# Batch 0 of a linear-attention kernel: keys and q loaded ahead of all values, E and F as f32 over two hardware queues

## Chip, cores and metric

One core of one Trainium2 chip. The metric is the device time of one execution in microseconds (us). The kernel before takes 522.49 us (median of six runs in the rounds of the comparison; 522.26 in the three runs known when the prediction was made).

## The reference, cut to what matters

```python
k_proj = einsum('ks,bhsd->bhkd', E, k)          # E: 64 x 1024; k: 8 batches, 8 heads, 1024 x 64
v_proj = einsum('ks,bhsd->bhkd', F, v)
scores = (1 / sqrt(64)) * q @ k_proj^T          # 1024 x 64 for each head
attn   = softmax(scores)
x      = (attn @ v_proj), heads side by side    # 8192 x 512
h = x @ w_in                                    # 512 -> 2048
out = (h * clip(h + 3, 0, 6) / 6) @ w_out       # 2048 -> 512
```

The two large products (w_in, w_out) are nearly all of the work. Batch b + 1's attention is woven into the large products of batch b; only the attention of batch 0 has nothing to hide behind.

## The kernel before: the parts concerned

Heads are handled in four pairs. `busy(n)` is n matmuls of ones on ones, whose result nobody reads: fillers, meant to keep TensorE's clock up.

```python
ef_raw = consts.tile([P, S], bf16, name="ef_raw")
nc.gpsimd.dma_start(out=ef_raw[:KP], in_=E)            # f32 in memory, cast to bf16 on the way
nc.gpsimd.dma_start(out=ef_raw[KP:], in_=F)
# (cut) table load, ones
busy(8)
for n, j in (("k", 0), ("q", 0), ("v", 0), ("k", 1), ("q", 1), ("k", 2), ("q", 2), ("v", 1),
             ("k", 3), ("q", 3), ("v", 2), ("v", 3)):
    nc.gpsimd.dma_start(out=kqv[0][n][:, 2 * j:2 * j + 2], in_=kqv_dram[n][0][:, 2 * j:2 * j + 2])
# (cut) w_in, k/q/v of batch 1, w_out follow on the same queue
for so in range(SO):                                    # E and F turned, 128 rows together
    nc.tensor.transpose(ef_ps[:, so * P:(so + 1) * P], ef_si[:, so, :], ident)
nc.vector.tensor_copy(ef_t[0], ef_pv[:, 0])             # E's half; F's half by ScalarE
# (cut)
def by_pairs(self):
    keys(0)                                             # project, copy to kp
    self.q_out(0, self.q_transpose(0, pat)); self.keys_transposed(0, 2)
    busy(2); self.scores(0, pmm); busy(3)               # scores: matmuls, then exp on ScalarE
    vals(0)(); keys(1)
    self.q_out(1, self.q_transpose(1, pat))
    lns = logs(0, both)                                 # sums of exp (matmuls), ln on ScalarE
    self.keys_transposed(2, 2); busy(1)
    self.scores(1, pmm)
    recs = inverses(lns)                                # exp(-ln): behind the next pair's exp
    av = self.values(0, pat, both); busy(3)             # attn @ v_proj
    # (cut) pairs 2 and 3 alike: values of pair j - 1 or j - 2 between keys and scores of pair j
    rest = [vals(2)]; av = self.values(2, pat, one); out(2, av, recs)
    recs = inverses(logs(3, one)); rest.append(vals(3)); busy(1)
    av = self.values(3, pat, one); out(3, av, recs)     # x of the last pair
    for copy in rest: copy()
    busy(4)                                             # then the first large product
```

The softmax here doesn't subtract the row's maximum and nothing guards it: scores larger than these inputs give would overflow.

## Time and profile before

| | kernel before |
|---|---|
| median of 6 runs (lowest, highest) | 522.49 us (521.59, 522.92) |
| span of the profiled run, granted clock | 520.9 us, 0.999 |
| TensorE busy | 506.9 us, 97% |
| first keys projected | 7.20 us |
| first large matmul (the plateau) | 28.11 us |
| from there to the end of the span | 492.8 us |

Most lines that carry the reading are in the prediction. One more, the scores of the last pair, is the row of the old order with which the changed kernel is compared below:

```profile
23.41 0.41 PE L196 MATMUL mm<-qTp,kT 64*64 64x256 bf16 x8
```

The busy tenths of VectorE and of the DMA engines in slices of 13 us show that VectorE has room in the first two slices (1 and 5 tenths busy) while the loads fill their engines (8 and 9):

```profile
DVE  1568636444363453554454354534525544444420
...
DMA  8999993993049711695119931298111110011112
```

### The profile page before, as it was taken

The page shows a single profiled execution, that of the slowest core. Times are in us where ns is not written, and L with a number is a line of the kernel's source. Part 1 is how long each engine was busy: PE and PEld are TensorE (multiplying, and loading weights), DVE is VectorE, ACT ScalarE, POOL GpSimd, SP SyncE. Part 2 cuts the span into 40 slices and gives each one's busy share as a digit, 9 for nine tenths or more (in the row PEclk, how much of TensorE's full clock was granted, in tenths as well). Part 3 has the DMA queues.
Part 4 walks back from the last instruction along what each step waited for, and adds up shares of the span by engine and source line. Part 5 has one row for each costly group of instructions (what it writes and reads, how often), then busy time and mean ns, then how long its engine had stood idle before and what let it go on. Part 6 is the DMA issues. An engine that isn't in the chain of part 4 may idle for free.

```text
span 520.9 us, 7264 instructions
## 1 busy us (share of the span) xinstructions
PE 506.9 (97%) x2806; PEld 225.1 (43%) x2858; DVE 238.5 (46%) x378; ACT 283.9 (55%) x517; POOL 36.3 (7%) x55
## 2 busy tenths in 40 slices
PE   6899999999999999999999999999999999999996
PEld 3444444444444444444444444444444444444443
DVE  1568636444363453554454354534525544444420
ACT  2677485676446654568437664466635664444431
POOL 7620000100020000200002000200000000000000
PEclk9999999999999999999999999999999999999999
DMA  8999993993049711695119931298111110011112
GB/s 131 203 207 207 207 181 117 190 151 97 22 77 211 145 43 42 117 196 121 42 30 170 176 81 42 63 204 168 42 40 32 40 42 28 34 42 41 40 42 81
DMA packets 67443, 53.95 MB, mean 104 GB/s; under 512 B 29776, under 2 KB 59216, under 8 KB 67408
## 3 DMA queue, kind: packets, MB, share of 16 engines
q0 software_dynamic: 30016, 29.63, 35.6%
q1 hardware_dynamic: 37248, 23.73, 17.3%
q8 instruction: 22, 0.36, 0.3%
q10 hardware_dynamic: 144, 0.13, 0.1%
q14 instruction: 13, 0.11, 0.1%
HBM read 59.24 MB, written 16.78 MB: 146 GB/s over the span
## 4 chain that ended last, share of the span: by engine, by line
PE 94%; DMA 2%; issue 1%; DVE 1%; POOL 1%; ACT 1%; DVEq 0%; ACTq 0%; POOLq 0%
PE mm L393 43%; PE mm L402 41%; PE at L210 3%; PE at L150 3%; DMA q<-in_q_dram 2%; PE at L196 1%; PE mm L84 1%; PE at L180 1%; DVE qTp L187 0%; DVE xT L232 0%; DVE vp L162 0%; PE mm L210 0%; PE mm L196 0%; ACT aT L201 0%; POOL k L95 0%
## 5 line engine op out<-in xcount | busy, mean ns | idle before, releaser
L397 DVE SCALAR_TENSOR_TENSOR g<-r,mm 128x512 bf16<-128x512 f32 x256 | 173.4, 686 | 218.6 <-ACT r L396 218.4
L393 PE MATMUL mm<-xT,w_in_sb 128*128 128x512 bf16 x1000 | 233.1, 380 | 2.6 <-issue 1.9
L402 PE MATMUL mm<-w_out_sb,g 128*128 128x512 bf16 x999 | 230.1, 380 | 1.5 <-issue 0.3
L396 ACT ACTIVATE r<-mm 128x512 f32<-128x512 f32 x256 | 152.3, 603 | 62.6 <-PE mm L393 61.3
L393 PEld LDWEIGHTS <-w_in_sb 128*128 128x128 bf16 x1024 | 96.8, 98 | 125.6 <-issue 14.1
L402 PEld LDWEIGHTS <-g 128*128 128x128 bf16 x1024 | 98.9, 98 | 119.4 <-issue 2.2
L416 ACT COPY o_sb<-mm 128x512 f32<-128x512 f32 x63 | 36.9, 586 | 147.6 <-PE mm L402 144.7
L232 DVE TENSOR_TENSOR xT<-at,rec 128x512 bf16<-128x512 f32 x56 | 38.2, 684 | 16.5 <-ACT rec L228 15.4
L228 ACT ACTIVATE rec<-ln 128x512 f32<-128x512 f32 x64 | 40.4, 640 | 0.1
L223 ACT ACTIVATE ln<-at 128x512 f32<-128x512 f32 x59 | 32.7, 617 | 2.4 <-PE at L210 2.3
L201 ACT ACTIVATE aT<-at 128x512 bf16<-128x512 f32 x56 | 29.2, 612 | 0.9 <-PE at L196 0.9
L358 POOL COPY mark<-kT 1x1 bf16<-1x1 bf16 x5 | 0.9, 177 | 276.4 <-DMA kT<-kp 276.4
L150 PE MATMUL at<-k,ef_t 128*64 128x512 bf16 (+1 forms) x88 | 15.9, 323 | 1.1 <-DMA k<-in_k_dram 1.1
L150 PE MATMUL at<-v,ef_t 128*64 128x512 bf16 (+1 forms) x88 | 15.9, 324 | 0.0
L150 PEld LDWEIGHTS <-ef_t 128*64 128x64 bf16 x176 | 9.6, 109 | 11.4 <-issue 5.9
L162 DVE CAST vp<-at 64x512 bf16<-64x512 f32 (+1 forms) x21 | 11.3, 541 | 4.0 <-PE at L150 3.0
L210 PE MATMUL at<-aT,vp 64*64 64x512 bf16 x112 | 12.3, 379 | 0.5 <-DVE vp L162 0.4
L210 PE MATMUL at<-aT,ones 64*64 64x512 bf16 x118 | 12.7, 400 | 0.0
L84 PE MATMUL mm<-ones 128*128 128x512 bf16 x31 | 10.9, 446 | 1.6 <-DVE ones L77 1.5
L157 DVE CAST kp<-at 64x512 bf16<-64x512 f32 (+1 forms) x21 | 10.2, 522 | 4.3 <-PE at L150 4.3
L210 PEld LDWEIGHTS <-ones 64*64 64x64 bf16 x128 | 3.9, 103 | 13.4 <-issue 13.1
L196 PEld LDWEIGHTS <-kT 64*64 64x64 bf16 x256 | 5.8, 106 | 8.0 <-issue 5.1
(44 smaller groups left out, 94.8 us busy)
## 6 DMA issues: line engine op xcount, KB each, us to landing
out_dram<-o_sb SPq DMA_DIRECT2D x63, 256.0 KB, 2.0
q<-in_q_dram POOLq DMA_DIRECT2D x7, 1024.0 KB, 9.5
k<-in_k_dram POOLq DMA_DIRECT2D x7, 1024.0 KB, 15.0
v<-in_v_dram POOLq DMA_DIRECT2D x7, 1024.0 KB, 19.9
w_out_sb<-in_moe_w_out_dram POOLq DMA_DIRECT2D x4, 512.0 KB, 27.7
w_in_sb<-in_moe_w_in_dram POOLq DMA_DIRECT2D x3, 512.0 KB, 12.6
k<-in_k_dram POOLq DMA_DIRECT2D x4, 256.0 KB, 8.1
q<-in_q_dram POOLq DMA_DIRECT2D x4, 256.0 KB, 8.6
```

The costliest lines, as they stand in the source:

```text
L84: nc.tensor.matmul(ps, ones[:, :P], ones, start=True, stop=True)
L150: nc.tensor.matmul(ps[e * KP:(e + 1) * KP], ef_t[e][:, so, :], kqv[self.b]["kv"[e]][:, hs, so, :], start=(so == 0), stop=(so == SO - 1))
L201: nc.scalar.activation(self.aT[j][:, r].rearrange("p a n -> p (a n)"), tiles[r], AF.Exp, scale=scale)
L210: nc.tensor.matmul(tiles[t][c:c + D].rearrange("p (r n) -> p r n", r=2), stationary(r, 2 * j + a), self.aT[j][r:r + KP, :, a, :], start=Tr ...
L223: nc.scalar.activation(ln, den, AF.Ln)
L228: nc.scalar.activation(rec, ln, AF.Exp, scale=-1.0)
L232: nc.vector.tensor_mul(self.xT[:, j, t, :], av, rec)
L393: nc.tensor.matmul(h_ps, w_in_sb[:, ko, fo * P:(fo + 1) * P], xT[:, ko, t, :], start=(ko == 0), stop=(ko == KO - 1))
L396: nc.scalar.activation(r, h_ps, AF.Relu, bias=0.5, scale=1.0 / 6.0)
L397: nc.vector.scalar_tensor_tensor(g[:, fo, :], r, 1.0, h_ps, op0=ALU.min, op1=ALU.mult)
L402: nc.tensor.matmul(o_ps, g[:, fo, c * P:(c + 1) * P], w_out_sb[:, fo, :], start=(fo == 0), stop=(fo == FO - 1))
L416: nc.scalar.copy(o_sb, o_ps)
```

## The change

Its intent: TensorE should get through keys, q, scores and sums of all pairs as fast as the loads come, with values and products behind; and E and F should leave GpSimd's queue, so that every casting load starts earlier. Cut to its core:

```diff
-    ef_raw = consts.tile([P, S], bf16, name="ef_raw")
-    nc.gpsimd.dma_start(out=ef_raw[:KP], in_=E)
-    nc.gpsimd.dma_start(out=ef_raw[KP:], in_=F)
+    ef_f32 = consts.tile([P, S], f32, name="ef_f32")
+    nc.sync.dma_start(out=ef_f32[:KP], in_=E)
+    nc.scalar.dma_start(out=ef_f32[KP:], in_=F)
-    busy(8)
+    busy(12)
-    for n, j in (("k", 0), ("q", 0), ("v", 0), ("k", 1), ... ("v", 2), ("v", 3)):
+    for n, j in [(n, j) for j in range(KO) for n in ("k", "q")] + [("v", j) for j in range(KO)]:
+    nc.vector.tensor_copy(ef_raw[:, :S // 2], ef_f32[:, :S // 2])
+    nc.scalar.copy(ef_raw[:, S // 2:], ef_f32[:, S // 2:])
     # by_pairs, new body (the old one is cut)
+            for j in range(KO):
+                keys(j)
+                if j > 0: self.scores(j - 1, pmm)
+                busy(1)
+                self.keys_transposed(2 * j, 2)
+                self.q_out(j, self.q_transpose(j, pat))
+                busy(1)
+                if j > 0:
+                    den = self.sums(j - 1, pmm, ts)          # ts: both halves for pair 0, else one
+                    lns = {t: self.log(den[t]) for t in ts}
+                    recs[j - 1, 0] = reciprocal(lns[0], opool, "o_sb")
+                    ...                                      # and recs[0, 1] for pair 0
+                    busy(1)
+            self.scores(KO - 1, pmm)
+            for j in range(KO):
+                copy = vals(j); copy(0); ...                 # second copy at once for pair 0, else later
+                av = self.values(j, pat, range(NB) if j == 0 else (0,))
+                self.scaled(j, 0, av[0], recs[j, 0])
+                busy(1)
+                ...                                          # j == 0: second half, sums of pair 3, busy(1)
+            for copy in rest: copy(1)
+            busy(2)
```

More of the change, by code (lines that the diff above doesn't have):

```diff
@@ L92 @@
     kqv = {0: {n: raw_tile(n) for n in ("k", "q", "v")}}
-    for n, j in (("k", 0), ("q", 0), ("v", 0), ("k", 1), ("q", 1), ("k", 2), ("q", 2), ("v", 1),
-                 ("k", 3), ("q", 3), ("v", 2), ("v", 3)):
+    for n, j in [(n, j) for j in range(KO) for n in ("k", "q")] + [("v", j) for j in range(KO)]:
         nc.gpsimd.dma_start(out=kqv[0][n][:, 2 * j:2 * j + 2],
@@ L119 @@
     ef_t = [consts.tile([P, SO, KP], bf16, name=f"ef_t{e}") for e in range(2)]
+    ef_raw = consts.tile([P, S], bf16, name="ef_raw")
+    nc.vector.tensor_copy(ef_raw[:, :S // 2], ef_f32[:, :S // 2])
+    nc.scalar.copy(ef_raw[:, S // 2:], ef_f32[:, S // 2:])
     ef_si = ef_raw.rearrange("r (si so) -> r so si", so=SO)
@@ L236, in by_pairs, with pair @@
         def by_pairs(self):
-            both, one = (0, 1), (0,)
+            def pair(j):
+                return slice(2 * j, 2 * j + 2)
             def keys(j):
@@ L241, in keys @@
                 for so in range(SO):
-                    self.project(pk, 0, slice(2 * j, 2 * j + 2), so)
-                self.keys_out(pk, slice(2 * j, 2 * j + 2))
+                    self.project(pk, 0, pair(j), so)
+                self.keys_out(pk, pair(j))
             def vals(j):
@@ L247, in vals @@
                 for so in range(SO):
-                    self.project(pv, 1, slice(2 * j, 2 * j + 2), so)
-                self.values_out(pv, slice(2 * j, 2 * j + 2), copies=(0,))
-                return lambda: self.values_out(pv, slice(2 * j, 2 * j + 2), copies=(1,))
-            def logs(j, ts):
-                den = self.sums(j, pmm, ts)
-                return {t: self.log(den[t]) for t in ts}
-            def out(j, av, recs):
-                for t in recs:
-                    self.scaled(j, t, av[t], recs[t])
@@ L260, in inverses @@
-            def inverses(lns):
-                return {t: self.inverse(lns[t]) for t in lns}
-            keys(0)
-            self.q_out(0, self.q_transpose(0, pat))
-            self.keys_transposed(0, 2)
-            busy(2)
-            self.scores(0, pmm)
-            busy(3)
-            vals(0)()
-            keys(1)
-            self.q_out(1, self.q_transpose(1, pat))
-            lns = logs(0, both)
-            self.keys_transposed(2, 2)
-            busy(1)
-            self.scores(1, pmm)
@@ L277, in by_pairs @@
-            recs = inverses(lns)
-            av = self.values(0, pat, both)
-            busy(3)
-            keys(2)
-            self.q_out(2, self.q_transpose(2, pat))
-            lns = logs(1, one)
-            self.keys_transposed(4, 2)
-            busy(1)
-            out(0, av, recs)
-            self.scores(2, pmm)
-            recs = inverses(lns)
-            vals(1)()
-            busy(3)
-            keys(3)
-            lns = logs(2, one)
-            busy(2)
-            self.qT[3] = att.tile([P, 2, TOK], bf16, tag="qTp", name="qTp")
@@ L296, in by_pairs @@
-            halves = [self.q_transpose(3, pat, (a,)) for a in range(2)]
-            self.keys_transposed(6, 2)
-            nc.vector.tensor_copy(self.qT[3][:, 0], halves[0])
-            nc.scalar.copy(self.qT[3][:, 1], halves[1])
-            av = self.values(1, pat, one)
-            out(1, av, recs)
-            busy(2)
-            self.scores(3, pmm)
-            recs = inverses(lns)
-            busy(2)
-            rest = [vals(2)]
-            av = self.values(2, pat, one)
-            out(2, av, recs)
@@ L309, in by_pairs, with reciprocal @@
-            recs = inverses(logs(3, one))
-            rest.append(vals(3))
-            busy(1)
-            av = self.values(3, pat, one)
-            out(3, av, recs)
-            for copy in rest:
-                copy()
-            busy(4)
+                    self.project(pv, 1, pair(j), so)
+                return lambda a: self.values_out(pv, pair(j), copies=(a,))
+            def reciprocal(ln, pool, tag):
+                rec = pool.tile([P, TOK], f32, tag=tag, name=tag)
+                nc.scalar.activation(rec, ln, AF.Exp, scale=-1.0)
+                return rec
@@ new lines, in by_pairs @@
+            recs = {}
+            for j in range(KO):
+                keys(j)
+                if j > 0:
+                    self.scores(j - 1, pmm)
+                busy(1)
+                self.keys_transposed(2 * j, 2)
+                self.q_out(j, self.q_transpose(j, pat))
+                busy(1)
+                if j > 0:
+                    ts = range(NB) if j == 1 else (0,)
+                    den = self.sums(j - 1, pmm, ts)
+                    lns = {t: self.log(den[t]) for t in ts}
+                    recs[j - 1, 0] = reciprocal(lns[0], opool, "o_sb")
+                    if j == 1:
+                        recs[0, 1] = self.inverse(lns[1])
+                    busy(1)
@@ new lines, in by_pairs @@
+            self.scores(KO - 1, pmm)
+            rest = []
+            for j in range(KO):
+                copy = vals(j)
+                copy(0)
+                if j == 0:
+                    copy(1)
+                else:
+                    rest.append(copy)
+                av = self.values(j, pat, range(NB) if j == 0 else (0,))
+                self.scaled(j, 0, av[0], recs[j, 0])
+                busy(1)
+                if j == 0:
+                    self.scaled(0, 1, av[1], recs[0, 1])
+                    den = self.sums(KO - 1, pmm, (0,))
+                    recs[KO - 1, 0] = reciprocal(self.log(den[0]), opool, "o_sb")
+                    busy(1)
@@ L319, in second_block @@
+            for copy in rest:
+                copy(1)
+            busy(2)
         def second_block(self):
```

## The prediction

> **What bounds the kernel now.** I read the busy slices first, then the chain that ended last, then the timeline of the first 30 us. The slices of TensorE (PE; one digit is the busy share of 13 us in tenths):
>
> ```profile
> PE   6899999999999999999999999999999999999996
> ```
>
> and the chain by engine:
>
> ```profile
> PE 94%; DMA 2%; issue 1%; DVE 1%; POOL 1%; ACT 1%; DVEq 0%; ACTq 0%; POOLq 0%
> ```
>
> TensorE is full from 26 us to the end, and 94% of the chain is its work. The change touches only what stands before that plateau: the attention of batch 0. The instruction order confirms that nothing behind it is edited. So the question is one instant: when does the first large matmul, the one with w_in_sb, start? What moves it, moves the end by as much, since the group mm<-xT,w_in_sb shows only 2.6 us of idle ahead of 1000 matmuls.
>
> Three strands lead to that instant. The first is the loads. GpSimd queues them (start, length, then in brackets how long it sat and for what):
>
> ```profile
> 1.24 0.66 POOL L73 DMA_DIRECT2D ef_raw<-in_E_dram  x1 [0.79 <-POOLq L479]
> ...
> 2.41 0.74 POOL L95 DMA_DIRECT2D k<-in_k_dram  x1
> ...
> 11.57 0.70 POOL L95 DMA_DIRECT2D v<-in_v_dram  x1 [1.31 <-DMA v<-in_v_dram]
> ...
> 23.11 0.87 POOL L104 DMA_DIRECT2D v<-in_v_dram  x1 [0.42 <-DMA v<-in_v_dram]
> ```
>
> From v2 on (11.57) each waits until an earlier load has landed, eight loads back: v2 for v0, v3 (12.86) for k1, and so on to 23.11, which v3 released. These starts are landing times, late by about 0.25. The pace is 1.29 us for one load of 256 KB, about 203 GB/s as written, double that as read: the DMA engines are the limit of this strand. By issue and time to landing: k0 7.1, q0 9.2, v0 11.3, k1 12.6, q1 13.8, k2 15.1, q2 16.4, v1 17.7, k3 19.0, q3 20.3, v2 21.5, v3 22.9. The first two queue entries are E and F, so k0 is queued 1.17 us after E (2.41 - 1.24).
>
> The second strand is the start of TensorE:
>
> ```profile
> 1.46 3.52 PE L84 MATMUL mm<-ones 128*128 128x512 bf16 x8 [1.46 <-DVE ones L77]
> ...
> 7.20 0.61 PE L150 MATMUL at<-k,ef_t 128*64 128x128 bf16 x8 [1.06 <-DMA k<-in_k_dram]
> ```
>
> Eight fillers at 0.43 each, then E and F transposed (from 5.02), then the first keys, held until k0 has landed.
>
> The third is the end of the stage:
>
> ```profile
> 25.86 0.64 PE L150 MATMUL at<-v,ef_t 128*64 128x128 bf16 x8
> ...
> 27.42 0.69 DVE L232 TENSOR_TENSOR xT<-at,rec 128x512 bf16<-128x512 f32 x1 [0.57 <-PE at L210]
> ...
> 28.11 3.62 PE L393 MATMUL mm<-xT,w_in_sb 128*128 128x512 bf16 x16
> ```
>
> Values of the last pair projected, copied (26.55), multiplied (26.90), scaled (end 27.42 + 0.69 = 28.11), fillers, and the plateau at 28.11. From the start of the last projection to its xT is 2.25 us. Data is no limit there: v3 had landed 3 us before 25.86. The first chunks of w_in_sb landed near 24.4 and 25.7.
>
> [...] So I credit the two queues with the 1.17 us of GpSimd's queue, not with bandwidth; the trace of before has no E or F on another queue to test it. [...] fillers at 0.43 us until 4.87 (3.41 us after 1.46), then 0.215 (three fillers and the switch to the next weights in 0.75 us, 11.20 to 11.95). Hence the four fillers more cost about 4 x 0.215 = 0.86, not 4 x 0.43. [...] in this trace the ScalarE rows come in program order.
>
> **The change part by part.**
>
> *Loads.* Queue slots shift by -1.17, and v0 and v1 leave the front. Keys and q: k0 5.9, q0 8.0, k1 (slot of v0) 11.3 - 1.17 = 10.1, q1 11.4, k2 12.6, q2 13.9, k3 15.2, q3 16.5; values 17.8, 19.1, 20.3, 21.7. q3 comes 3.8 us earlier. With loads alone as the limit the last scores could start near 16.5 + 0.56 + 0.10 + 0.69 + 0.05 = 17.9.
>
> *E and F.* Each is 256 KB as f32. An output store of 256 KB from SP shows 2.0 us from issue to landing; queued near 0.8, both land near 3 to 3.5; the copies (ScalarE 128x512 is 0.58) end near 4.2. But twelve fillers stand ahead on TensorE: 4.87 + 0.86 = 5.75 instead of 5.02. The transposes end 0.7 later, ef_t is copied at 6.5 to 6.9 (0.42), and keys of pair 0 start at 6.95, against 7.20: the early k0 is worth only 0.25 here.
>
> *Pairs 0 to 3, keys and q.* Durations from the trace: projection of a pair 0.56 on TensorE and its copy 0.67 after its start, two kp copies 0.48, score matmuls 0.34 and the first exponential 0.45 after their start, q transposes 0.56, copy of q 0.69, sums 0.33, the logarithm 0.45 after their start. In the new order the scores of pair 0 stand behind keys of pair 1, so wait for k1: 10.1 + 0.56 = 10.66. Now ScalarE's groups, from the old kernel:
>
> ```profile
> 14.89 1.08 ACT L223 ACTIVATE ln<-mm 128x512 f32<-128x512 f32 x2 [2.49 <-PE mm L210]
> ...
> 15.88 1.09 ACT L201 ACTIVATE aT<-mm 128x512 bf16<-128x512 f32 x2
> ...
> 16.85 1.15 ACT L228 ACTIVATE rec<-ln 128x512 f32<-128x512 f32 x2
> ```
>
> Old order: logarithms, then the next exponentials, then reciprocals. New order: exponentials, logarithms, reciprocals, and only then the next exponentials; and TensorE takes the sums of a pair, which need its exponentials, before the keys of the next pair but one. This is a ring: exponentials 11.11 to 12.20, sums at 12.26, two logarithms 12.71 to 13.79, two reciprocals to 14.94, exponentials of pair 1 to 16.03, sums of pair 1 at 16.08, filler, keys of pair 3 at 16.73 (k3 had landed at 15.2), scores of pair 2 at 17.29, exponentials 17.76 to 18.85, sums of pair 2 at 18.9, logarithm and reciprocal to 20.58, exponentials of pair 3 to 21.67. TensorE has the scores of pair 3 done at 19.83: 1.6 us after what the loads allow.
>
> *Values.* The phase starts at 19.83; v0 is there. Pair 0: projection, both copies 20.50 to 21.09, values to 21.36, filler 21.58, then sums of pair 3, which need 21.67; another filler; pair 1 at 22.37. For later pairs: copy at +0.67, done +0.96, values +1.01, +0.33, filler and switch +0.32 = 1.66 each. So pair 2 at 24.03, pair 3 at 25.69, its xT at 25.69 + 2.25 = 27.94, where before had 28.11. The two last fillers end at 26.70 + 0.33 + 0.43 = 27.46; three matmuls of the plateau (0.65) fit before the fourth needs that xT, so the plateau runs as if started at 27.46: 0.65 earlier. Where the scheduler's dependency holds all of xT, the gain is 0.17.
>
> Sum: between -0.2 and -0.65, centre -0.45: 522.26 - 0.45 = 521.8.
>
> **The rivals.** (1) Loads are the only limit: TensorE and ScalarE keep up, the value phase starts at 18.2, xT at 26.3, time 520.4. For it: 3.8 us of earlier q3. Against it: the ring on ScalarE, 2.23 us of logarithms and reciprocals between two exponentials. (2) The early loads are no faster than before, as two f32 transfers (512 KB written, not 256) run against k0: k1 at 10.9, ring and end 0.8 later, time 522.6. [...] against it: the bytes read are the same and start earlier. (3) The value phase is longer than 1.66 per pair, as the copy waits behind the scaling on VectorE (0.69): 3 x 0.3 gives 522.7. The old trace has such a cycle in 1.56 (24.30 to 25.86), against it. (4) Gaps of about 0.9 us on TensorE let its clock fall again; 3.4 us at half rate would put off up to 1.7 us of work, near 523.5. The old trace had a gap of 1.5 us before 9.32 and stayed fast; unlikely.
>
> **Range and chances.** The loads' limit bounds the gain at 2 us, (2) and (3) the loss at 1; runs of before spread by 1.3. Range 520.3 to 523.0. Two per cent is 10.4 us, a third of the whole stage: 1% either way.
>
> **What would show it.** Right: first keys near 7.0, TensorE waiting for k1 near 10, ScalarE without a gap from about 12.7 to 16.0, sums of pair 1 ended by the exponential, value phase near 19.8, plateau near 27.5. Wrong: k1 landing a microsecond off 10.1; sums of pair 1 before 15.5; E and F landing after 5 us; a plateau start off by over 1 us; or new waits after 30 us, which I hold for none.

The 1.17 us of the queue and the fillers at 0.43 and 0.215 us are read off the trace of before (k0 queued at 2.41, E at 1.24; the fillers' weight loads 0.43 apart from 1.86 to 4.00, three fillers and the switch in 0.75 from 11.20). That the two queues were credited with these 1.17 us and nothing more was assumption and was not shown, nor was the reason for casting E and F on the core. The traces show that in both kernels GpSimd issues every load that casts. That the DMA engines are the limit of the loads is read off their busy digits, 8 and 9 tenths in the first two slices. Rival (4) is a hypothesis that no trace had shown yet (e_first and f_vals_ahead later had falls of the clock behind gaps of 1.20 and of 0.44 and 0.85 us): its 3.4 us is the time for which the first fillers ran at 0.43 in the trace of before (3.41), its gap of 0.9 us an assumption.

## The result, and the profile after

The changed kernel takes 522.0 us (median of six, 521.64 to 522.21), the kernel before 522.49. The ratio is 0.9991, with a 95% interval of 0.9978 to 1.0004, so it does not exclude 1. (Ratios here are the mean time of one kernel's fast runs over that of the other's fast runs of the same rounds, so not quite the ratio of the medians.) The forecast was 521.8. An interval from 1.1 us of gain to 0.2 of loss could not have told the forecast gain of 0.45 from none, so the number alone confirms little; the rows of the traces have to.

| | before | after |
|---|---|---|
| first keys projected | 7.20 | 8.00 |
| keys of pair 1 projected | 12.62 | 10.14 |
| last scores | 23.41 | 19.43 |
| plateau | 28.11 | 27.79 |
| span of the profiled run | 520.9 | 520.4 |

The last scores come 4.0 us earlier, and 0.3 us is left of it at the plateau. Each column is one execution, and both lie above the mean of their kernel at full clock: the profiled one of before took 522.67 (mean 521.93, in the sets below), that of the changed kernel 522.21 (mean 521.96). So tenths between the columns are not all due to the edit. The page of the changed kernel has the same plateau, with a first slice busier by a tenth on TensorE and on the DMA engines:

```profile
PE   7899999999999999999999999999999999999997
...
DMA  9999993993049611795119831298111110111112
```

The chain by engine: the share of the loads (DMA) fell from 2% to 1%, so that ScalarE, VectorE and the loads now stand level behind TensorE.

```profile
PE 94%; ACT 1%; DVE 1%; issue 1%; DMA 1%; DVEq 0%; ACTq 0%
```

The timeline's first 11 us: SP and ACT issue E and F, GpSimd starts with k0, and what the first keys now wait for is named in the brackets:

```profile
0.74 0.58 SPq L73 DMA_DIRECT2D ef_f<-in_E_dram  x1
0.74 0.58 ACTq L74 DMA_DIRECT2D ef_f<-in_F_dram  x1
...
1.24 0.82 POOL L94 DMA_DIRECT2D k<-in_k_dram  x1 [0.79 <-POOLq L459]
...
6.10 0.62 ACT L121 CAST ef_raw<-ef_f 128x512 bf16<-128x512 f32 x1 [3.47 <-DMA ef_f<-in_F_dram]
...
6.78 0.71 PE L125 MATMUL at<-ident,ef_raw 128*128 128x128 bf16 x8 [1.16 <-ACT ef_raw L121]
...
8.00 0.63 PE L152 MATMUL at<-k,ef_t 128*64 128x128 bf16 x8
...
9.63 0.72 POOL L94 DMA_DIRECT2D v<-in_v_dram  x1 [0.59 <-DMA k<-in_k_dram]
...
10.14 0.63 PE L152 MATMUL at<-k,ef_t 128*64 128x128 bf16 x8
```

F landed at 6.04, 0.4 us behind the fillers' end (5.62); the copies, transposes and first keys follow one another from there to 8.00. GpSimd's issue at 9.63 was released by k1, which had landed at 9.3, but TensorE reached k1 only at 10.14.

The middle of the stage, with ScalarE's exponentials, logarithms and next exponentials, the sums of pair 1 on TensorE, the last scores, and the first projection of values:

```profile
11.22 1.09 ACT L203 ACTIVATE aT<-mm 128x512 bf16<-128x512 f32 x2 [2.66 <-PE mm L198]
...
12.81 1.09 ACT L225 ACTIVATE ln<-mm 128x512 f32<-128x512 f32 x2 [0.50 <-PE mm L212]
...
14.82 1.08 ACT L203 ACTIVATE aT<-mm 128x512 bf16<-128x512 f32 x2
...
15.96 0.40 PE L212 MATMUL mm<-aT,ones 64*64 64x512 bf16 x2 [0.70 <-ACT aT L203]
...
19.43 0.41 PE L198 MATMUL mm<-qTp,kT 64*64 64x256 bf16 x8 [0.25 <-DVE qTp L189]
...
19.77 0.63 PE L152 MATMUL at<-v,ef_t 128*64 128x128 bf16 x8
```

The bracket in the row at 15.96 is the ring of the prediction: TensorE sat idle for 0.70 us until ScalarE had the exponentials of pair 1, and these had stood behind two reciprocals. And the end of the stage, row for row as shown for before:

```profile
25.78 0.64 PE L152 MATMUL at<-v,ef_t 128*64 128x128 bf16 x8
...
26.80 0.40 PE L212 MATMUL at<-aT,vp 64*64 64x512 bf16 x2 [0.39 <-DVE vp L164]
...
27.31 0.69 DVE L234 TENSOR_TENSOR xT<-at,o_sb 128x512 bf16<-128x512 f32 x1 [0.57 <-PE at L212]
...
27.79 3.62 PE L373 MATMUL mm<-xT,w_in_sb 128*128 128x512 bf16 x16
```

### The profile page after: what moved, and what is told of

Its sections match the earlier page's. It is cut to its first block, busy times and chain, and to the rows that moved or that the text cites. A ratio compares the mean times of both kernels' runs of the same rounds, so it can differ in the third digit from the quotient of the medians.

```text
span 520.4 us, 7264 instructions
## 1 busy us (share of the span) xinstructions
PE 506.5 (97%) x2804; PEld 225.7 (43%) x2856; DVE 239.5 (46%) x379; ACT 284.0 (55%) x517; POOL 35.4 (7%) x53
## 4 chain that ended last, share of the span: by engine, by line
PE 94%; ACT 1%; DVE 1%; issue 1%; DMA 1%; DVEq 0%; ACTq 0%
PE mm L373 43%; PE mm L382 41%; PE at L212 4%; PE at L152 3%; PE at L198 1%; DMA ef_f<-in_F_dram 1%; PE mm L84 1%; PE at L182 1%; ACT aT L203 0%; PE mm L212 0%; DVE vp L164 0%; ACT ln L225 0%; PE mm L198 0%; DVE kp L159 0%; ACT rec L230 0%
## 5 line engine op out<-in xcount | busy, mean ns | idle before, releaser
L234 DVE TENSOR_TENSOR xT<-at,rec 128x512 bf16<-128x512 f32 x52 | 35.5, 683 | 15.4 <-ACT rec L230 15.4
L230 ACT ACTIVATE rec<-ln 128x512 f32<-128x512 f32 x60 | 38.0, 640 | 0.1
L189 DVE COPY qTp<-at 128x1024 bf16<-128x1024 bf16 x8 | 5.5, 691 | 7.5 <-PE at L182 7.5
```

What stands on the lines that cost most here:

```text
L230: nc.scalar.activation(rec, ln, AF.Exp, scale=-1.0)
L234: nc.vector.tensor_mul(self.xT[:, j, t, :], av, rec)
```

## The experiments

Twelve kernels, all correct, in three sets of four. Each set ran on one chip, beside the kernel before. "Full clock" counts the executions with a granted clock of 0.999 or 1.0; the other executions of the same kernel are longer, with one exception (522.16 at 0.998 in the kernel before). The ratio takes in the executions of lower clock too. Most executions of the kernel before are such, so the ratio flatters the kernels that keep their clock, and the last column is the fairer comparison. No run differs from the kernel before by as much as 1%: what is weighed here are differences inside a stage of 28 us.

| run | plateau, us | median, us | ratio (95%) | full clock | mean at full clock |
|---|---|---|---|---|---|
| a_order_only | 28.50 | 523.02 | 1.0000 (0.9985 to 1.0015) | 6 of 6 | 522.99 |
| b_ef_only | 26.20 | 520.60 | 0.9955 (0.9941 to 0.9969) | 5 of 5 | 520.62 |
| c_no_tail | 26.85 | 521.32 | 0.9969 (0.9956 to 0.9983) | 5 of 5 | 521.36 |
| d_ring | 26.80 | 521.20 | 0.9966 (0.9952 to 0.9980) | 5 of 5 | 521.18 |
| kernel before, same rounds | | 522.82 | | 2 of 11 | 522.24 |
| e_first | 30.80 | 523.93 | 1.0037 (1.0019 to 1.0055) | 1 of 6 | 523.28 |
| f_vals_ahead | 26.43 | 520.35 | 0.9969 (0.9952 to 0.9985) | 4 of 6 | 520.28 |
| g_all | 25.26 | 520.81 | 0.9986 (0.9960 to 1.0011) | 3 of 6 | 520.33 |
| h_ef_no_tail | 25.37 | 520.06 | 0.9958 (0.9943 to 0.9973) | 5 of 5 | 520.28 |
| kernel before, same rounds | | 522.64 | | 5 of 12 | 521.87 |
| i_halves | 27.92 | 522.28 | 0.9989 (0.9973 to 1.0004) | 6 of 6 | 522.30 |
| j_ahead_warm | 26.49 | 520.67 | 0.9958 (0.9944 to 0.9973) | 6 of 6 | 520.71 |
| k_best | 24.68 | 520.19 | 0.9949 (0.9933 to 0.9966) | 6 of 6 | 520.12 |
| l_before_warm | 27.70 | 522.45 | 0.9996 (0.9980 to 1.0013) | 5 of 6 | 522.48 |
| kernel before, same rounds | | 523.07 | | 3 of 11 | 521.81 |

### The change in its two parts

**a_order_only**: the new order, E and F by the old path; the twelve fillers of the changed kernel stay.

```diff
-    ef_f32 = ...; nc.sync.dma_start(...E); nc.scalar.dma_start(...F)
+    ef_raw = ...; nc.gpsimd.dma_start(...E); nc.gpsimd.dma_start(...F)
-    nc.vector.tensor_copy(ef_raw[...]); nc.scalar.copy(ef_raw[...])
```

> The new order of loads and pairs alone; E and F cast by GpSimd's queue as in the kernel before (twelve fillers kept). Theory (the queue part is worth over a microsecond of loads, of which the late landing of F gives most back): k1 is queued 1.1 us later and lands between 10.4 and 11.3 instead of 9.3, the first keys start near 7.2 instead of 8.0, but the scores of pair 0 stand behind k1 and start between 11.0 and 11.9 instead of 10.77; plateau 28.0 to 28.9 (changed kernel 27.79), time 522.2 to 523.1. Rival (E and F on other queues do nothing, F lands too late, the order is all): time and plateau of the changed kernel, 522.0 and 27.8.

```profile
8.20 0.61 PE L149 MATMUL at<-k,ef_t 128*64 128x128 bf16 x8 [0.42 <-DMA k<-in_k_dram]
...
10.92 0.63 PE L149 MATMUL at<-k,ef_t 128*64 128x128 bf16 x8 [0.55 <-DMA k<-in_k_dram]
```

k1 was used at 10.92, scores of pair 0 at 11.49, plateau 28.50, 523.02: inside what the theory said, and against the rival. One part missed: the first keys came at 8.20, not near 7.2, because k0 landed at 8.1, where the same load had landed at 7.1 in the kernel before. **The order by itself gains nothing**; against the two full-clock runs of before in these rounds it is 0.75 us slower.

**b_ef_only**: the kernel before with the new path of E and F and twelve fillers.

```diff
-    nc.gpsimd.dma_start(out=ef_raw[:KP], in_=E); nc.gpsimd.dma_start(out=ef_raw[KP:], in_=F)
+    nc.sync.dma_start(out=ef_f32[:KP], in_=E); nc.scalar.dma_start(out=ef_f32[KP:], in_=F)
+    nc.vector.tensor_copy(ef_raw[...]); nc.scalar.copy(ef_raw[...])
-    busy(8)
+    busy(12)
```

> The kernel before with E and F as f32 by two hardware queues and twelve fillers, old order. Theory: all loads of k, q, v land 1.1 us earlier; first keys 8.0 instead of 7.20, but q of pair 1, for which TensorE waited until 13.85, lands at 12.7, and from there TensorE is busy: plateau 27.0 (before 28.11), time 521.4, faster than the changed kernel; then the new order costs half a microsecond. Rival (only the order gains): 522.5, plateau 28.1, first keys late and nothing won back.

More than expected: plateau 26.20, 520.60, the ratio 0.9955. Its timeline: q of pair 1 is turned at 11.90, where before it was 13.89, and ScalarE does the exponentials of pair 1 (13.97) ahead of the reciprocals of pair 0 (14.94):

```profile
11.90 0.62 PE L183 MATMUL at<-ident,q 128*128 128x128 bf16 x8
...
13.97 1.09 ACT L204 ACTIVATE aT<-mm 128x512 bf16<-128x512 f32 x2
...
14.94 1.15 ACT L231 ACTIVATE rec<-ln 128x512 f32<-128x512 f32 x2
```

So q1 came 2.0 us earlier, not 1.1, and all that follows on TensorE moved with it (1.91 at the plateau). **Half of the change, alone, is worth 1.6 us at full clock; the other half takes it back.** Of the whole change this says: the queue part pays and the new order costs. The two do not simply add: at the plateau the new order costs 0.4 with E and F on the old path (28.11 to 28.50) and 1.6 with them on the new one (26.20 to 27.79).

### What holds the stage in the changed kernel

**c_no_tail**: the last two fillers taken out.

```diff
             for copy in rest:
                 copy(1)
-            busy(2)
```

> The changed kernel without the last two fillers ahead of the plateau. If a matmul of the plateau waits only for the part of xT that it reads: start at 27.36 instead of 27.79, the fourth at 28.01 where xT of pair 3 is ready at 28.00, so the plateau gains 0.4 and the time is 521.6. If it waits for all of xT: start near 28.05, time 522.2 or unchanged.

```profile
5.59 0.62 ACT L121 CAST ef_raw<-ef_f 128x512 bf16<-128x512 f32 x1 [2.96 <-DMA ef_f<-in_F_dram]
...
7.49 0.63 PE L152 MATMUL at<-k,ef_t 128*64 128x128 bf16 x8
...
26.29 0.40 PE L212 MATMUL at<-aT,vp 64*64 64x512 bf16 x2 [0.39 <-DVE vp L164]
...
26.85 3.66 PE L372 MATMUL mm<-xT,w_in_sb 128*128 128x512 bf16 x16
```

From the last product to the plateau there is now 0.56 us (26.29 to 26.85) against 0.99 in the changed kernel (26.80 to 27.79): 0.43, as expected, so the first matmuls of the plateau do not wait for the whole of xT. Other traces show it directly: in the changed kernel they start at 27.79, where the last part of xT is done at 28.00, and in h_ef_no_tail four of them start from 25.37 on, while that part is written from 25.55 to 26.24. But the plateau came 0.94 earlier. The other 0.51 is no part of the edit: in this execution F landed 0.51 earlier (copies at 5.59, not 6.10), and every later row, 7.49 against 8.00 to 26.29 against 26.80, stands 0.51 earlier. Unasked, it shows that between these two executions the landing of F carried through to the plateau one for one. In the seven traces in which E and F are issued this way F landed between 5.5 and 6.0; that of the changed kernel is the latest.

**d_ring**: reciprocals behind the next pair's exponentials.

```diff
                 if j > 0:
                     self.scores(j - 1, pmm)
+                invert()                        # reciprocals of the pair before that
-                    recs[j - 1, 0] = reciprocal(lns[0], opool, "o_sb")
-                    if j == 1: recs[0, 1] = self.inverse(lns[1])
+                    pending.append((j - 1, lns))
             self.scores(KO - 1, pmm)
+            invert()
```

> The changed kernel with each pair's reciprocals behind the next pair's exponentials on ScalarE, nothing else moved. Theory (the ring on ScalarE holds TensorE): exponentials of pair 1 start near 14.05 instead of 14.82, sums of pair 1 at 15.2 instead of 15.96, values from 19.0 instead of 19.77, plateau 27.0, time 521.2. Rival (TensorE's own order or the loads hold it): values from 19.7, time 522.0.

```profile
13.83 1.08 ACT L203 ACTIVATE aT<-mm 128x512 bf16<-128x512 f32 x2 [0.15 <-PE mm L198]
...
14.97 0.40 PE L212 MATMUL mm<-aT,ones 64*64 64x512 bf16 x2
```

The exponentials of pair 1 now follow their scores at once, and the sums at 14.97 no longer wait. First keys to first values: 7.78 to 18.78 is 11.00 us, where the changed kernel has 8.00 to 19.77, 11.77. The ring cost 0.77, as worked out; the time, 521.20, is the 521.2 expected, of which 0.22 is again F's landing (first keys at 7.78).

**e_first**: E ahead of F, each in two halves of 32 rows on both queues; F copied and turned behind the q of pair 0.

```diff
-    nc.sync.dma_start(out=ef_f32[:KP], in_=E); nc.scalar.dma_start(out=ef_f32[KP:], in_=F)
+    for e, src in enumerate((E, F)):
+        nc.sync.dma_start(out=ef_f32[e][:HR], in_=src[:HR])
+        nc.scalar.dma_start(out=ef_f32[e][HR:], in_=src[HR:])
-    busy(12)
+    busy(9)
+    projection(0)                               # copy and turn E; F in by_pairs behind q of pair 0
```

> The changed kernel with E ahead of F: each in two halves of 32 rows on both hardware queues, E copied and transposed alone, F behind the q of pair 0; nine fillers at the start, not twelve. Theory (the landing of F holds the first keys, and they hold the stage): E lands near 4.5 instead of F at 6.0, first keys at k0's landing near 6.8 instead of 8.0, keys of pair 1 at 9.4 instead of 10.14 (k1 lands 9.3), values from 19.0, plateau 27.05, time 521.3. Rival (k1 or the ring alone hold it): values from 19.7, time 522.0.

A miss, and of my own making. E landed at 4.1 and the first keys started at 7.09, but I had put F's copy behind the copy of q on VectorE, which ran the two in that order (9.11, then 9.72); TensorE stood idle for 1.20 us:

```profile
9.72 0.41 DVE L124 CAST ef_raw<-ef_f 64x512 bf16<-64x512 f32 x1
10.28 0.68 PE L129 MATMUL at<-ident,ef_raw 64*128 64x64 bf16 x8 [1.20 <-DVE ef_raw L124]
```

Then the clock fell. The stretches from 9 us on (length, then the busy time of PE, PEld, DVE, ACT, POOL; then the granted clock; DMA share and GB/s):

```profile
9.00:10.00 1.00, 0.08 (x2) 0.00 (x0) 0.89 (x2) 0.00 (x0) 0.44 (x2) 1.00 1.23 202
...
10.25:10.50 0.25, 0.22 (x4) 0.25 (x5) 0.00 (x0) 0.00 (x0) 0.25 (x1) 0.96 1.23 205
10.50:10.75 0.25, 0.25 (x7) 0.25 (x6) 0.00 (x0) 0.00 (x0) 0.19 (x1) 0.50 1.22 193
...
12.00:16.00 4.00, 4.00 (x30) 1.79 (x28) 1.40 (x4) 1.26 (x3) 2.25 (x3) 0.50 1.24 204
```

It stayed at 0.50 until past 17 us. That is the fourth rival of the prediction, in a kernel that was not meant to test it; five of six executions have a clock under 0.999. At full clock the one remaining run took 523.28, over a microsecond more than the changed kernel's mean (521.96, from other rounds). As far as one execution can tell, that is what the misplaced copy of F costs apart from the clock. It says nothing for or against the theory it was made for.

**i_halves**: the halves without the mistake; nothing else is moved.

```diff
+    for lo, src in ((0, E), (KP, F)):
+        nc.sync.dma_start(out=ef_f32[lo:lo + HR], in_=src[:HR])
+        nc.scalar.dma_start(out=ef_f32[lo + HR:lo + KP], in_=src[HR:])
```

> The changed kernel with E and F each as two loads of 32 rows, one on each hardware queue, nothing else. Theory (the landing of F holds the first keys, they hold the stage): F lands near 5.3, as it did in the run with E first, instead of 6.0; first keys at 7.2 instead of 8.0, keys of pair 1 at 9.35 (k1 lands 9.3) instead of 10.14, values from 19.0 instead of 19.77, plateau 27.0, time 521.2, granted clock 1.0. Rival (k1 or the ring holds it): values from 19.7, time 522.0.

```profile
7.10 0.63 PE L154 MATMUL at<-k,ef_t 128*64 128x128 bf16 x8
...
10.34 0.63 PE L154 MATMUL at<-k,ef_t 128*64 128x128 bf16 x8 [1.03 <-DMA k<-in_k_dram]
```

F landed at 5.0 and the first keys came 0.90 earlier, as expected, but in this execution k1 landed only at 10.3 (bracket), 1.0 later than in the changed kernel's, and the plateau was at 27.92. This profiled execution is the slowest of the six; the six times, 521.85 to 522.76, lie no lower than the changed kernel's, against the 521.2 expected. So F's landing holds the first keys, but freeing it alone hands the stage to k1, which in the changed kernel had landed only 0.8 us ahead of its use. Why k1 landed later here stays open.

### The values

**f_vals_ahead**: the next pair's values projected ahead of each product, no fillers between.

```diff
             for j in range(KO):
-                copy = vals(j); copy(0) ...
+                if j + 1 < KO:
+                    copy = vals(j + 1); copy(0); rest.append(copy)
                 av = self.values(j, ...)
                 self.scaled(j, 0, av[0], recs[j, 0])
-                busy(1)
     # (cut) the values of pair 0 ahead of the loop; the filler behind the sums of pair 3 goes too
-            busy(2)
+            busy(3)                             # the last fillers
```

> The changed kernel with the projection of the next pair's values put ahead of each pair's product, so that TensorE does not wait for the copy of vp, and without the fillers between; three fillers at the end. Theory (the value phase is one chain of projection, copy, product, 1.66 a pair): values from 19.77 as before, VectorE becomes the bound with about 1.0 a pair, last xT at 25.6 instead of 28.00, plateau 25.4 instead of 27.79, time 519.7. Rival (the loads of v or w_in_sb hold it): v3 lands near 22, w_in_sb near 23.3, plateau not under 27, time 521.5.

The plateau came at 26.43, not at the 25.4 expected. VectorE became the bound, as the wait of the last product shows:

```profile
24.84 0.40 PE L212 MATMUL at<-aT,vp 64*64 64x512 bf16 x2 [0.85 <-DVE xT L234]
```

The last product starts at 24.84, 1.96 earlier than in the changed kernel, of which 0.22 is the earlier F. The four executions at full clock took 520.28 in the mean, about half a microsecond over the 519.7 expected; the profiled one, at 0.997, took 521.92: behind the idle gaps of 0.44 and 0.85 us the clock fell to 0.50 from 25.2 to 28.5 and the plateau started at half rate.

**j_ahead_warm**: the same with fillers in those gaps.

```diff
                     copy = vals(j + 1); copy(0); rest.append(copy)
+                    busy(1)
                 self.scaled(j, 0, av[0], recs[j, 0])
+                if 0 < j < KO - 1:
+                    busy(2)
```

> The run with the values projected ahead, plus fillers where TensorE waited for VectorE (one behind each projection, two behind each product of pairs 1 and 2). Theory (without fillers the clock falls in some executions: 0.996 and 0.997 in two of six there): the clock is 0.999 or 1.0 in all, plateau 25.8 to 26.0, all times 520.1 to 520.5. Rival (the fall has another cause): again a third of the executions near 521.9.

The clock is 0.999 or 1.0 in all six, as expected. But the fillers are not free: the last product starts at 25.50, not 24.84, the plateau at 26.49 (25.8 to 26.0 expected), and the six take 520.59 to 520.90 (520.1 to 520.5 expected), 0.4 above the full-clock runs without them. Six executions of six kept the clock, where four of six did, at a cost of about 0.4 us (the two ran on different chips).

### Versions, and the clock of the kernel before

**h_ef_no_tail**: b_ef_only without its last `busy(4)`.

```diff
             for copy in rest:
                 copy()
-            busy(4)
```

> The kernel before with E and F on the hardware queues, and its last four fillers taken away. Those stand between the last product (24.99) and the plateau (26.20); the last xT is ready at 26.2 and the fourth matmul needs it, so the plateau starts at 25.5 and gains 0.65: time 519.9 to 520.0, against 520.6 with them. If the fillers stand beside other waiting: 520.6.

Close to what was expected (25.5, and 519.9 to 520.0): plateau 25.37, four of five times from 520.00 to 520.15 (the fifth 521.12): 0.5 below b_ef_only, on another chip.

**g_all**: d_ring, e_first and f_vals_ahead together, no fillers at the end.

```diff
+    # the edits of d_ring, e_first and f_vals_ahead, as shown there
-            busy(2)                             # the last fillers
```

> The three together: reciprocals behind the exponentials, E ahead of F, values projected ahead, no fillers at the end. If the gains add: values from 18.3, last xT at 24.1; v3 lands near 22 and needs 2.2 to its xT, so not under 24.2; plateau near 23.9 to 24.3, time 518.4. If the loads take over sooner, 519.5.

The gains did not add to the 518.4 expected: it carries the misplaced copy of F (keys of pair 1 at 10.84), and three of six executions lost their clock. At full clock 520.33.

**k_best**: d_ring, i_halves and j_ahead_warm together, one filler at the end.

```diff
+    # the edits of d_ring, i_halves and j_ahead_warm, as shown there
-            busy(2)
+            busy(1)                             # the last fillers
```

> Halves of E and F, reciprocals behind the exponentials, values ahead with fillers, one filler at the end. If the gains add: values from 18.2, last product held by VectorE or by v3 (lands near 22): last xT at 24.5, plateau 24.0 to 24.5, time 518.5, under the 520.06 of the kernel before with E and F on the hardware queues and no tail. If the loads slow down or the clock falls: 520.

```profile
18.33 1.08 PE L154 MATMUL at<-v,ef_t 128*64 128x128 bf16 x16
...
24.12 0.40 PE L214 MATMUL at<-aT,vp 64*64 64x512 bf16 x2 [0.32 <-DVE xT L236]
```

Values from 18.33, last product at 24.12 held by VectorE, plateau 24.68, 3.1 before the changed kernel's. The profiled execution was the fastest of six (519.56); the median is 520.19, 1.7 above what I expected. k1 had landed at 8.9 in this trace and at 10.3 in that of i_halves, with the same first loads; I take the spread of the six (519.56 to 520.49) for that, but no trace of a slower one shows it. k_best and h_ef_no_tail have the lowest medians and kept a full clock in all executions; at full clock they are 1.7 and 1.6 us below the kernel before in the same rounds. f_vals_ahead and g_all are as fast where they kept the clock (520.28 and 520.33), but did not always keep it. Between k_best and h_ef_no_tail, on different chips, I claim no order.

**l_before_warm**: the kernel before with four fillers behind the first keys, where TensorE waits for q0 (1.51 us, up to 9.32, in the trace of before).

```diff
             keys(0)
+            busy(4)
             self.q_out(0, self.q_transpose(0, pat))
```

> The kernel before with four fillers more, in the gap behind the first keys in which TensorE waits for q0 (8.0 to 9.3). They cost nothing on the path. Theory (this gap is where the clock of the kernel before falls in some executions, which then take 523 to 526): all clocks 0.999 or 1.0, all times 521.6 to 522.3, median some 0.5 under the kernel before of the same rounds. Rival (the falls come elsewhere): clocks of 0.992 to 0.997 as often as in the kernel before.

Five of six executions had the full clock, against three of eleven of the kernel before in the same rounds. That speaks for the gap as the place, but one (523.74 at 0.996) fell all the same, and the five others took 522.48 in the mean, more than the kernel before at full clock in these rounds (521.81, three executions). The theory had said all six at full clock and all times up to 522.3, so this is half a confirmation at best.

## Why the prediction was right, and where it was not

- **The time.** 521.8 forecast, 522.0 measured; -0.45 forecast, -0.49 in the medians, with an interval that does not exclude 0. The plateau was to gain between 0.17 and 0.65 and gained 0.32.
- **The loads: mis-sized.** The step "queue slots shift by -1.17" put k1 at 10.1; it landed at 9.3. From the third slot to q of pair 3 all came 1.9 to 2.0 earlier than before, not 1.17 (k1 released GpSimd's issue at 9.63, where v0 in the same slot had done so at 11.57); k0 and q0 only about 0.4 and 1.2 (6.7 and 8.0, where they were 7.1 and 9.2). The early half of the queue of before ran below its pace (129 and 175 GB/s in the microseconds from 8 to 10, against 206 and 205 in the changed kernel), and I shifted that lull along instead of expecting it to close. What caused the lull is not shown.
- **E and F: failed.** The step "both land near 3 to 3.5" rested on an output store of 256 KB, 2.0 us. E took 4.2 and F 5.3 us: landed at 4.94 and 6.04. The twelve fillers, which I had as the cause of the later first keys, ended ahead of F (5.62). First keys 8.00, not 6.95. The prediction's own list names "E and F landing after 5 us" as a sign that it is wrong; F did. Nor was its cost of the fillers a constant: the same twelve took 4.16 us here and 5.30 in a_order_only.
- **The two errors cancelled.** k1 came 0.8 too early and TensorE, which was to wait for it, came to it 0.8 after it had landed (9.3, 10.14), so the scores of pair 0 started at 10.77, where 10.66 was forecast. That is luck, a right number for a wrong reason; only the parts, b_ef_only (2.0 for the loads) and c_no_tail and i_halves (F holds the first keys), take it apart.
- **The ring: right.** Sums of pair 1 at 15.96 (forecast 16.08), values from 19.77 (19.83). d_ring undid it and got the 0.77 back.
- **The value phase: right.** Pair 3 at 25.78 (25.69), its xT at 28.00 (27.94); 1.67 a pair (1.66). f_vals_ahead shows that it was this chain and not the loads of v: with the loads issued in the same order its last product starts at 24.84, not 26.80.
- **The end: a miscount.** I had two fillers ahead of the plateau; the loop's own makes three. With 0.22 for it, and the last product 0.10 later than forecast (26.80, not 26.70), 27.46 becomes 27.79. c_no_tail settled the open question of that step, in favour of partial waits (0.56 us from the last product to the plateau, not 0.99).
- **Rivals.** The first (loads alone bound the stage) fell with d_ring and f_vals_ahead, the second (k1 at 10.9) with k1 at 9.3, the third with 1.67 a pair. The fourth, the clock, I dismissed because the one trace of before kept its clock (0.999, with a gap of 1.51 us). In the changed kernel it did not come true, but the ground was weak: the executions of before in three later sets did not all keep theirs: 24 of 34 show a granted clock under 0.999, six of them 0.992, at 523.76 to 526.29 us, while the changed kernel had 0.999 or 1.0 in all six. Where in the kernel before the clock falls, no trace of a slow execution shows.

How much of the -0.49 is the stage and how much the clock stays open. The 10 executions of the kernel before at full clock have a mean of 521.93, the six of the changed kernel 521.96: no gain; but they come from other rounds, which ran on three chips, and of the first rounds only the profiled run's clock of the kernel before is known.

So where did the expected gain of the change go? The queue part gave about 1.9 us at the plateau (b_ef_only). The new order gave it back: 1.6 at the plateau, 0.8 of it in the ring on ScalarE (d_ring), and about 0.2 of it is no cost of the order but the later F of that trace (first keys 8.00, in b_ef_only 7.77). The rest I put down to the value phase, which ran bare: projection, copy, product, with nothing left to put between, where the old order had keys, q and scores of the next pair. f_vals_ahead got 1.7 out of that phase, so it is large enough; that it is all of the rest is argued, not shown.

## What to carry to other kernels

Bringing work forward gains nothing where it only empties the place in which other waits were hidden (here the last scores came 4.0 us earlier and the plateau 0.3): count what stands between the waits in the new order. Where an engine runs its instructions in program order, as ScalarE ran the reciprocals (13.78, 14.30) ahead of the exponentials (14.82) in the changed kernel and VectorE the copy of q (9.11) ahead of F's (9.72) in e_first, look at what stands ahead of the one that the next engine waits for; here one pair of reciprocals ahead of the exponentials cost 0.8 us, and one copy in the wrong place about a microsecond (one execution at full clock, 523.28 against 521.96), and five of its six executions show a clock under 0.999. Try the parts of a change separately: a part may be worth more than the whole.

## Measured here, and not explained

- Idle gaps on TensorE of 1.20 us (e_first) and of 0.44 and 0.85 us with one product between (f_vals_ahead) came just ahead of a fall of the granted clock to 0.50, which lasted 6.8 and 3.4 us. Gaps of 1.51 us in the kernel before and of 1.03 in i_halves did not, in the executions profiled. So here a fall followed gaps shorter than one of 1.51 us that no fall followed; that the gaps caused the falls is not shown.
- In the changed kernel E's first bytes moved at 2.1, 0.8 us after its issuing instruction ended (1.4 after it began). Two equal loads, issued at the same moment (0.74) by SP and ACT, started 1.1 us apart: E's bytes moved from 2.1 to 4.1, F's from 3.2 to 5.2, and they landed at 4.94 and 6.04. In halves over both queues they landed at 4.0 and 5.0 (i_halves).
- Landing times spread from one execution to the next: the same third load of GpSimd's queue landed at 8.9 in one kernel and 10.3 in another (k_best, i_halves), and F at 5.5 or 6.0 in executions whose loads up to then are the same (c_no_tail, changed kernel).
